# Top-32 attention and an ELU feed-forward on one core: remainder queries by four heads, and a planned feed-forward

## The chip, the core and the metric

The kernel runs on one core of a Trainium2 chip. Its time is the device time of that core in microseconds (us). The kernel before takes 1917.3 us, the median of three runs from 1916.89 to 1917.46. The core has a matrix engine (TensorE, PE in the profile), a vector engine (VectorE, DVE), a scalar engine (ScalarE, ACT), GpSimd (POOL) and DMA queues. Each engine works through its own list of instructions in order and waits on semaphores for the others.

## What is computed

Attention over 8 batches and 8 heads, 576 queries and 576 keys of width 64, in which each query keeps its 32 largest scores, and then a feed-forward with an ELU between its two matrices (512 to 2048 to 512) over the 4608 rows:

```python
scores = scale * np.matmul(q, k.transpose(0, 1, 3, 2))
kth = np.partition(scores, -top_k, axis=-1)[..., -top_k:-top_k + 1]     # top_k = 32
scores = np.where(scores >= kth, scores, -1000000000.0)
scores = scores - np.max(scores, axis=-1, keepdims=True)
attn = np.exp(scores)
attn = attn / (np.sum(attn, axis=-1, keepdims=True) + 1e-09)
x = np.matmul(attn, v)            # (B, H, S, D), then to rows of B*S, columns of H*D
h = x @ w_in
g = np.where(h > 0.0, h, np.exp(np.minimum(h, 0.0)) - 1.0)
out = g @ w_out
```

The two weight matrices arrive as float64 and are turned into fp32 in the kernel, from their bits.

## The kernel before

**Attention in steps.** 576 queries are four tiles of 128 (query tiles 0 to 3) and a remainder of 64 (tile 4). A step is one query tile and one pair of heads (hp, four pairs). In a full step each of the two heads has 128 rows of 576 scores. In a step of the remainder the two heads share the 128 partitions, 64 rows each, so there is only one such block (`nh = 1`, `weight = 0.5`). There are 8 batches of 16 full and 4 half steps, 160 in all, with 288 blocks of 128 x 576 to select from.

Step n goes through a software pipeline. `scores` (lines 243 to 266) is issued two steps ahead: per head two matmuls of 288 keys (L252) into PSUM, and ACT's scaled copy to SBUF (L261). `select` (L268) finds the 32nd largest: four MAX8 (L277, L287) and three MATCH_REPLACE8 (L281) per head on DVE. `mask` (L290) is issued a step later: two small operations on POOL (L298, L300), then a steep Prelu and an exp with a running sum on ACT (L301, L302). `normalise` (L306) takes a reciprocal on DVE (L311) and multiplies on POOL (L313). Two steps later `trans` (L317) turns four chunks of 128 keys per head with TensorE (L326) and copies them (L331), `trans_rest` (L336) turns the last 64 keys of each head on its own into 64 partitions (L341, L342), and `attend` (L347) multiplies by the values (L360) for a group of one or two query tiles, and copies the result into a block's `xT` (L377).

**Feed-forward in blocks.** A block is one to three tiles of 128 tokens, in which all 512 columns of x are wanted. The first pair of batches has blocks of 1, 1, 2, 2 and 3 tiles, every later pair three blocks of 3. When a block's last attention is in, `ffn_pieces` appends its work to a list: 16 hidden pieces (four matmuls each, L390, Relu and Exp on ACT, L398 and L399, and a gate on DVE, L400), and four projection pieces per tile (four matmuls of 512 columns each, L411). PSUM has two buffers for these pieces (`ps_f`).

**What sets the order.** The program is written step by step; a scheduler then orders each engine's instructions under the pools' buffers. `feed` is called four times in a step: it adds credit, 8 units per full step and at most 16 in store, and issues pieces while the credit covers them. A hidden piece costs as many units as its block has tiles, a projection piece 3.8. Nothing is issued until the weights are decoded (`"g" in late`).

**Decoding of the weights.** 32 pieces of 512 KB are loaded and decoded by `decode_piece`, three integer operations on DVE, four on ACT and two on POOL each (lines 144 to 168), called by `hook`, which `select` calls four times per head, eight per full step. Four buffers (`raw`) hold loads; after the last piece their space goes to the hidden activations (`g`).

Of the kernel before, what the change touches and what calls it, by code (L numbers as in the profile page):

```python
# [18 lines left out]
FEED = 8.0  # L19
# [17 lines left out]
class Block:  # L37


    def __init__(self, slots):  # L40
        self.slots = slots
        self.xT = None
        self.gT = []
        self.left = 0
        self.tiles = [[] for _ in range(slots)]
# [10 lines left out]
class Step:  # L56


    def __init__(self, t, hp, group, at):
        self.t, self.hp = t, hp  # L60
        self.group, self.at = group, at
        self.nh = 1 if t.rem else 2
        self.weight = 0.5 if t.rem else 1.0
# [3 lines left out]
def kernel(  # L67
# [44 lines left out]
    rawpool = raws.enter_context(tc.tile_pool(name="raw", bufs=4))  # L112
# [13 lines left out]
    def weight(i):  # L126
        per = dff // WN
        if i < NC * per:
            c, f = divmod(i, per)
            src = moe_w_in[c * P : (c + 1) * P, 2 * f * WN : 2 * (f + 1) * WN]  # L130
            return src, w_in[:, c, f * WN : (f + 1) * WN]
# [12 lines left out]
    def convert_first(i):  # L144
# [13 lines left out]
        nc.scalar.activation(e, ef, AF.Relu, scale=-(2.0**23), bias=span[:])  # L158
        nc.gpsimd.tensor_tensor(mf, mf, lof, ALU.add)
# [10 lines left out]
    decode = []  # L170

# [9 lines left out]
    def decode_piece(i):  # L181
        if i < 2 * NF:
            if i + 3 < 2 * NF:
                load_weight(i + 3)
            convert_first(i)
        if i > 0:
            convert_last(i - 1)

# [16 lines left out]
    def load_v(b, hp):  # L205
        t = kvpool.tile([P, 2, J + 1, D], FP32, tag="vT", name="vT")
        for hh in range(2):
            h = 2 * hp + hh
            nc.sync.dma_start(
                t[:, hh, 0:J, :],  # L210
                v[b, h, 0:JP, :].rearrange("(p j) d -> p j d", j=J),
            )
        nc.sync.dma_start(
            t[0:R, :, J, :],
            v[b, 2 * hp : 2 * hp + 2, JP:S, :].rearrange("h p d -> p h d"),
        )
# [26 lines left out]
    def scores(u):  # L243
        t = u.t
        kq = kqT[t.b, u.hp]
        q0 = t.qt * P
        u.sc = scpool.tile([P, 2, S], FP32, tag="sc", name="sc")
        ps = ps_sc.tile([P, 2, 2, 512], FP32, tag="s", name="scps")
        for half in range(2):
            for i in range(2):  # L250
                rows = slice(i * D, i * D + R) if t.rem else slice(0, P)
                nc.tensor.matmul(  # L252
                    ps[rows, i, half, 0:HS],
                    kq[i * D : (i + 1) * D, 1, q0 : q0 + t.ql],
                    kq[i * D : (i + 1) * D, 0, half * HS : (half + 1) * HS],
# [3 lines left out]
        for i in range(2):  # L259
            rows = slice(i * D, i * D + R) if t.rem else slice(0, P)  # L260
            nc.scalar.activation(  # L261
                u.sc[rows, 0 if t.rem else i, :].rearrange("p (a s) -> p a s", a=2),
                ps[rows, i, :, 0:HS],
                AF.Copy,
                scale=scale,
            )

    def select(u, i):  # L268
        if i >= u.nh:
            return  # L270
# [5 lines left out]
        hook()  # L276
# [3 lines left out]
        for r in range(TOP_K // 8 - 1):  # L280
# [7 lines left out]
            hook()  # L288

    def mask(u, i):  # L290

        if i >= u.nh:
            return
        if i == 0:
            u.den = small.tile([P, 2], FP32, tag="den", name="den")
        sc, low, top = u.sc[:, i, :], u.last[:, i, 7:8], u.first[:, i, 0:1]
# [9 lines left out]
    def normalise(u):  # L306
        nh = u.nh
        den = small.tile([P, 2], FP32, tag="dene", name="dene")
        nc.gpsimd.tensor_scalar_add(den[:, 0:nh], u.den[:, 0:nh], EPS)
        rec = small.tile([P, 2], FP32, tag="rec", name="rec")  # L310
        nc.vector.reciprocal(rec[:, 0:nh], den[:, 0:nh])  # L311
        for i in range(nh):
# [4 lines left out]
    def trans(u):  # L317

        g = u.group
        if g.et is None:  # L320
            n = len(g.tiles)
            g.et = etpool.tile([P, 2 * J + 2, n, P], FP32, tag="et", name="et")
        for i in range(u.nh):
            ps = ps_t.tile([P, JP], FP32, tag="t", name="eps")
            for c in range(J):
                nc.tensor.transpose(  # L326
                    ps[:, c * P : (c + 1) * P],
                    u.sc[:, i, c * P : (c + 1) * P],
                    ident[:],
                )  # L330
            nc.scalar.copy(  # L331
                g.et[:, i * J : (i + 1) * J, u.at, :],
                ps[:].rearrange("p (c q) -> p c q", c=J),
            )

    def trans_rest(u):  # L336

        g = u.group
        ps = ps_t.tile([P, JP], FP32, tag="t", name="eps")
        for i in range(u.nh):  # L340
            nc.tensor.transpose(ps[0:R, i * P : (i + 1) * P], u.sc[:, i, JP:S], ident[:])  # L341
        nc.scalar.copy(  # L342
            g.et[0:R, 2 * J : 2 * J + u.nh, u.at, :],
            ps[0:R, 0 : u.nh * P].rearrange("p (c q) -> p c q", c=u.nh),
        )

    def attend(g):  # L347
        t, hp = g.tiles[0], g.hp
        et, vt = g.et, vT[t.b, hp]
        n = sum(x.ql for x in g.tiles)  # L350
        ps = ps_t.tile([P, JP], FP32, tag="t", name="avps")
        for c in range(J + 1):
            for i in range(2):
                keys = slice(0, P if c < J else R)
                if t.rem:
                    w = et[keys, 2 * J if c == J else c, 0, i * R : (i + 1) * R]
                else:
                    w = et[keys, 2 * J + i if c == J else i * J + c, :, :]
                    w = w.rearrange("p a q -> p (a q)")
                nc.tensor.matmul(  # L360
                    ps[i * D : (i + 1) * D, 0:n],
                    vt[keys, i, c, :],
                    w,
                    start=(c == 0),
                    stop=(c == J),
                )
        c0 = 0
        tiles = list(g.tiles)
        while tiles:
            blk, lo = tiles[0].block, tiles[0].cols.start  # L370
# [199 lines left out]
```

## Time and profile before

| | before |
|---|---|
| time, median of 3 | 1917.3 us |
| span of the profiled run | 1915.4 us |
| TensorE busy | 1709.2 us, 89% |
| VectorE busy | 1615.8 us, 84% |
| ScalarE busy | 1169.8 us, 61% |
| GpSimd busy | 447.2 us, 23% |
| mean granted TensorE clock | 0.948 |
| hidden matmuls (L390) | 1792 instructions, 544.5 us |
| projection matmuls (L411) | 1152 instructions, 534.2 us |
| MAX8 and MATCH_REPLACE8 (L277, L281, L287) | 2016 passes of 754 to 761 ns |

The profile is one execution seen by the hardware profiler. A row of the timeline gives the start, the length, the engine, the line, the operation with its tiles and shapes, and in brackets how long the engine had been idle and what ended that. Matmuls overlap in the array, so the length of one matmul row says less than the distance from its start to the next row's start. A single-precision matmul is recorded as two instructions. The granted clock is the share of full speed at which TensorE ran.

### The profile page before, as it was taken

What the parts mean: (1) busy time and instruction counts of PE and PEld (TensorE: products, weight loads), DVE (VectorE), ACT (ScalarE), POOL (GpSimd) and SP (SyncE); (2) the same over time, 40 slices, a digit from 0 to 9 for tenths busy, and PEclk for the clock granted to TensorE, in tenths of its full rate; (3) what the DMA queues carried; (4) which work ended last, traced back from release to release, by engine and by line L of the source; (5) the groups of instructions that cost most, each with busy time, mean ns of one, the idle gap of its engine ahead of it and who ended that gap; (6) DMA issues with size and microseconds to landing.
All of it is one profiled execution on the core that took longest, in us unless ns stands there. A gap on an engine that the chain in (4) does not pass through costs nothing.

```text
span 1915.4 us, 24954 instructions
## 1 busy us (share of the span) xinstructions
PE 1709.2 (89%) x7984; PEld 946.7 (49%) x7984; DVE 1615.8 (84%) x3360; ACT 1169.8 (61%) x2453; POOL 447.2 (23%) x1096
## 2 busy tenths in 40 slices
PE   4028999999999999899989999999999999999999
PEld 2015656465554455455454455455555455445553
DVE  7999989999799998996999777997899777999310
ACT  6677667576666776575566466566566566557330
POOL 4774212222122222221222111221122211222000
PEclk7557999999899999999999999999999999999999
DMA  6430011000200110001100010000100000000000
GB/s 175 150 130 3 19 31 32 18 13 19 56 1 12 38 31 19 12 13 43 37 1 6 24 44 19 12 18 19 49 13 0 25 19 19 7 12 1 12 6 17
DMA packets 100610, 56.14 MB, mean 29 GB/s; under 512 B 83584, under 2 KB 91776, under 8 KB 100480
## 3 DMA queue, kind: packets, MB, share of 16 engines
q1 hardware_dynamic: 100480, 54.55, 10.3%
q8 instruction: 64, 1.05, 0.2%
q14 instruction: 66, 0.54, 0.1%
HBM read 45.09 MB, written 9.44 MB: 28 GB/s over the span
## 4 chain that ended last, share of the span: by engine, by line
DVE 56%; PE 31%; ACT 8%; issue 2%; POOL 1%; DMA 1%; SPq 0%; POOLq 0%; ACTq 0%; DVEq 0%
DVE wk L281 22%; DVE m L287 20%; PE hps L390 11%; PE ops L411 8%; DVE m L277 7%; PE scps L252 5%; PE avps L360 3%; DVE gT L400 3%; ACT sc L301 2%; PE eps L326 2%; ACT sc L261 2%; ACT sc L302 1%; DVE raw L164 1%; DVE raw L154 1%; DVE raw L151 1%
## 5 line engine op out<-in xcount | busy, mean ns | idle before, releaser
L287 DVE MAX8 m<-wk 128x8 f32<-128x576 f32 x864 | 631.9, 761 | 4.1
L390 PE MATMUL hps<-xT,w_in 128*128 128x384 f32 (+2 forms) x1792 | 544.5, 451 | 16.3 <-DVE gT L400 15.2
L411 PE MATMUL ops<-w_out,gT 128*128 128x512 f32 x1152 | 534.2, 604 | 0.0
L281 DVE MATCH_REPLACE8 wk<-m,wk 128x576 f32<-128x576 f32 x576 | 432.4, 754 | 0.0
L301 ACT ACTIVATE sc<-sc,neg 128x576 f32<-128x576 f32 x288 | 223.1, 775 | 336.5 <-POOL neg L298 336.0
L390 PEld LDWEIGHTS hps<-xT,w_in 128*128 128x128 f32 x1792 | 310.9, 192 | 196.0 <-DVE gT L400 31.0
L411 PEld LDWEIGHTS ops<-w_out,gT 128*128 128x128 f32 x1152 | 208.7, 192 | 223.1 <-issue 219.1
L252 PE MATMUL scps<-kqT 64*128 64x288 f32 (+1 forms) x1280 | 255.4, 456 | 17.4 <-ACT sc L261 15.8
L298 POOL TENSOR_SCALAR neg<-m 128x1 f32<-128x1 f32 x288 | 62.8, 218 | 847.2 <-DVE m L287 845.9
L277 DVE MAX8 m<-sc 128x8 f32<-128x576 f32 x288 | 215.7, 758 | 51.9 <-ACT sc L261 51.5
L313 POOL TENSOR_SCALAR sc<-sc,rec 128x576 f32<-128x576 f32 x288 | 214.0, 753 | 116.6 <-DVE rec L311 93.3
L302 ACT ACTIVATE sc<-sc,gap 128x576 f32<-128x576 f32 x288 | 223.4, 776 | 15.4 <-ACT sc L301 1.5
L360 PE MATMUL avps<-et,vT 128*64 128x256 f32 (+5 forms) x2000 | 205.9, 342 | 26.3 <-ACT et L342 25.6
L281 DVE MATCH_REPLACE8 wk<-m,sc 128x576 f32<-128x576 f32 x288 | 216.6, 754 | 0.0
L326 PE MATMUL eps<-ident,sc 128*128 128x128 f32 x1152 | 173.2, 284 | 48.1 <-ACT xT L377 23.5
L261 ACT ACTIVATE sc<-scps 128x576 f32<-128x576 f32 (+1 forms) x320 | 192.6, 641 | 28.9 <-PE scps L252 27.7
L400 DVE SCALAR_TENSOR_TENSOR gT<-n,hps 128x384 f32<-128x384 f32 (+2 forms) x224 | 109.9, 491 | 116.7 <-ACT n L399 115.0
L326 PEld LDWEIGHTS eps<-ident,sc 128*128 128x128 f32 x1152 | 133.4, 145 | 124.5 <-issue 70.7
L331 ACT COPY et<-eps 128x512 f32<-128x512 f32 x288 | 159.9, 585 | 51.4 <-PE eps L326 50.5
L360 PEld LDWEIGHTS avps<-et,vT 128*64 128x64 f32 (+1 forms) x2000 | 113.7, 141 | 135.2 <-issue 48.2
L252 PEld LDWEIGHTS scps<-kqT 64*128 64x128 f32 (+1 forms) x1280 | 121.0, 186 | 104.3 <-issue 58.2
L398 ACT ACTIVATE n<-hps 128x384 f32<-128x384 f32 (+2 forms) x224 | 98.3, 439 | 119.7 <-PE hps L390 118.1
(41 smaller groups left out, 969.1 us busy)
## 6 DMA issues: line engine op xcount, KB each, us to landing
kin<-in_k_dram SPq DMA_DIRECT2D x64, 128.0 KB, 2.7
qin<-in_q_dram SPq DMA_DIRECT2D x64, 128.0 KB, 2.8
raw<-in_moe_w_in_dram SPq DMA_DIRECT2D x16, 512.0 KB, 4.6
vT<-in_v_dram SPq DMA_DIRECT2D x64, 128.0 KB, 2.1
raw<-in_moe_w_out_dram SPq DMA_DIRECT2D x16, 512.0 KB, 3.2
out_dram<-osb SPq DMA_DIRECT2D x32, 256.0 KB, 2.3
kin<-in_k_dram SPq DMA_DIRECT2D x32, 32.0 KB, 2.5
qin<-in_q_dram SPq DMA_DIRECT2D x32, 32.0 KB, 2.5
```

Source lines behind the costliest of these rows:

```text
L252: nc.tensor.matmul(ps[rows, i, half, 0:HS], kq[i * D : (i + 1) * D, 1, q0 : q0 + t.ql], kq[i * D : (i + 1) * D, 0, half * HS : (half + 1) ...
L261: nc.scalar.activation(u.sc[rows, 0 if t.rem else i, :].rearrange("p (a s) -> p a s", a=2), ps[rows, i, :, 0:HS], AF.Copy, scale=scale,)
L277: nc.vector.max(m, sc)
L281: nc.vector.match_replace(wk[:], m, cur, TAKEN)
L287: nc.vector.max(m, cur)
L301: nc.scalar.activation(sc, sc, AF.Prelu, bias=neg[:], alpha=STEEP)
L302: nc.scalar.activation(sc, sc, AF.Exp, bias=gap[:], accum_out=u.den[:, i : i + 1])
L313: nc.gpsimd.tensor_scalar(u.sc[:, i, :], u.sc[:, i, :], rec[:, i : i + 1], 1.0, ALU.mult, ALU.mult)
L326: nc.tensor.transpose(ps[:, c * P : (c + 1) * P], u.sc[:, i, c * P : (c + 1) * P], ident[:],)
L360: nc.tensor.matmul(ps[i * D : (i + 1) * D, 0:n], vt[keys, i, c, :], w, start=(c == 0), stop=(c == J),)
L390: nc.tensor.matmul(ps[:, 0:n_tok], w_in[:, i, f * P : (f + 1) * P], blk.xT[:, i, 0:n_tok], start=(i == 0), stop=(i == NC - 1),)
L411: nc.tensor.matmul(blk.o[:], blk.gT[f // NG][:, f % NG, s * P : (s + 1) * P], w_out[:, f, :], start=(f == 0), stop=(f == NF - 1),)
```

## The change

Five things are changed together.

1. **Four heads per step of the remainder queries.** A step of tile 4 now takes four heads: two blocks of 128 rows, each made of 64 rows of one head and 64 of another. A batch has two such full steps instead of four half ones, 144 steps in all. `nh` and `weight` go.
2. **Last keys side by side.** Scores are taken as 512 keys and then 64 keys per head. The first head's last 64 keys and the second head's last 64 keys lie next to each other, so that nine chunks of 128 columns cover both heads; `turn` replaces `trans` and `trans_rest`, and nine wide transposes replace eight wide and two narrow ones.
3. **Blocks of two and three tiles.** The first pair of batches has blocks of 1, 1, 2, 1, 2 and 2 tiles, the later pairs 2, 2, 3 and 2; the remainder comes before the last two query tiles in every odd batch.
4. **A plan in place of the credit.** From the step at which each block becomes ready (`ready`) and the work of all blocks before it, `feed` computes the slowest rate that still finishes each block before the next is ready, and issues pieces at that rate. Costs are 1.1, 1.85 and 2.7 for a hidden piece of one, two and three tiles and 3.55 for a projection piece. Decoding is called half as often (four pieces per step), with the first matrix decoded column block by column block and three load buffers, and the first block may start on the weights decoded so far, with its own small buffer (`early`). The first eight steps run without the software pipeline's delay (`tight`).
5. **Gates queued late.** A hidden piece no longer issues its gate; it is put into `gates`, and issued when two are waiting, at the next `feed`, or before a projection.

The core of the diff:

```diff
+HIDDEN = {1: 1.1, 2: 1.85, 3: 2.7}
+PROJECT = 3.55
...
+        if t.rem:
+            rows = [(4 * hp, 0), (4 * hp + 2, 0), (4 * hp + 3, 1), (4 * hp + 1, 1)]
...
-    rawpool = raws.enter_context(tc.tile_pool(name="raw", bufs=4))
+    early = raws.enter_context(tc.tile_pool(name="early", bufs=1))
+    rawpool = raws.enter_context(tc.tile_pool(name="raw", bufs=3))
...
-        ps = ps_sc.tile([P, 2, 2, 512], FP32, tag="s", name="scps")
-        for half in range(2):
-            for i in range(2):
+        ps = ps_sc.tile([P, 4 * JP], FP32, tag="s", name="scps")
+        first = (0, 3 * JP - R)
+        main = (0, 3 * JP)
+        rest = (JP, 3 * JP - R)
+        for start, keys in ((main, slice(0, JP)), (rest, slice(JP, S))):
+            for h, i, rows in u.heads:
...
             nc.vector.max(m, cur)
-            hook()
+            if r != 1:
+                hook()
+                yield
...
+    def turn(u, chunks):
...
+        for c in range(n):
+            c0 = (chunks.start + c) * P
+            nc.tensor.transpose(ps[:, c * P : (c + 1) * P], sc[:, c0 : c0 + P], ident[:])
...
+            if len(gates) > 1:
+                close_gates()
             ps = ps_f.tile([P, dm], FP32, tag="f", name="hps")
...
-            nc.vector.scalar_tensor_tensor(
-                out=blk.gT[f // NG][:, f % NG, 0:n_tok],
-                in0=n[:, 0:n_tok], scalar=-1.0, in1=ps[:, 0:n_tok],
-                op0=ALU.add, op1=ALU.max,
-            )
+            gates.append((blk.gT[f // NG][:, f % NG, 0:n_tok], n, ps))
...
-            sizes = (1, 1, 2, 2, 3) if b == 0 else (3, 3, 3)
+            division = [(0,), (1,), (2, 3), (rest,), (4, 5), (6, 7)]
+            if b > 0:
+                division = [(0, 1), (2, 3), (rest, 4, 5), (6, 7)]
...
-        credit[0] = min(credit[0] + FEED * share * u.weight, 2 * FEED)
-        while ffn and credit[0] >= ffn[0][0]:
-            cost, piece = ffn.pop(0)
-            credit[0] -= cost
+        close_gates()
+        fed["at"] = max(fed["at"], n)
+        ahead = [(w - fed["sum"]) / (x - fed["at"]) for x, w in due if x > fed["at"]]
+        if ahead:
+            fed["over"] += max(0.0, share * min(ahead))
+        fed["at"] += share
+        while ffn and decoded[0] >= ffn[0][1] and 0.5 * ffn[0][0] <= fed["over"]:
+            cost, _, piece = ffn.pop(0)
+            fed["over"] -= cost
+            fed["sum"] += cost
             piece()
...
+        if n < tight:
+            for i in range(2):
+                passes = choose(n, i)
+                next(passes)
+                if i == 0:
+                    while closing:
+                        attend(closing.pop(0))
+                elif prev:
+                    normalise(prev)
+                    turn(prev, slice(0, J))
+                    turn(prev, slice(J, J + 1))
+                    turn(prev, slice(J + 1, 2 * J + 1))
+                feed(n, 0.25)
+                next(passes)
+                mask(cur, i)
+                feed(n, 0.25)
+            continue
```

## The prediction

> **What bounds the kernel now.** I read the page's first two parts, then the busy time of each engine in five stretches, then the order in time of TensorE around three moments, and last what VectorE waited for.
>
> ```profile
> PE 1709.2 (89%) x7984; PEld 946.7 (49%) x7984; DVE 1615.8 (84%) x3360; ACT 1169.8 (61%) x2453; POOL 447.2 (23%) x1096
> ...
> PE   4028999999999999899989999999999999999999
> ...
> DVE  7999989999799998996999777997899777999310
> ...
> PEclk7557999999899999999999999999999999999999
> ```
>
> TensorE (PE) is nearly empty in the first four slices and full afterwards; VectorE (DVE) is full in the first slices, has holes later and is empty for the last two. So one of them limits the start and the other the rest.
>
> ```profile
> 0.00:190.00 190.00, 72.14 (x395) 48.24 (x396) 174.06 (x291) 131.96 (x255) 111.65 (x129) 0.64 0.39 115
> 190.00:255.00 65.00, 64.76 (x369) 41.96 (x367) 63.30 (x149) 41.02 (x109) 15.30 (x43) 1.00 0.05 14
> 255.00:518.00 263.00, 252.51 (x1352) 151.49 (x1351) 239.03 (x521) 179.63 (x390) 57.10 (x167) 0.97 0.12 30
> 518.00:1787.00 1269.00, 1196.17 (x5448) 642.06 (x5447) 1124.67 (x2374) 788.32 (x1641) 260.83 (x754) 0.98 0.07 19
> 1787.00:1916.00 129.00, 123.61 (x426) 62.93 (x426) 14.70 (x28) 28.87 (x62) 2.29 (x6) 1.00 0.04 13
> ```
>
> Columns: PE, PE weight load, DVE, ACT, POOL busy, granted clock, DMA. The cuts are the moments at which 32, 80 and all 288 head-selections had been scored. PE idles 118 us up to 190, where weight decoding fills DVE; then 11 us to 518, 73 us of 1269 in the long stretch, 5 in the tail. In the long stretch DVE has 144 us free. The tail is feed-forward alone.
>
> ```profile
> 1014.30 1.24 PE L252 MATMUL scps<-kqT 64*128 64x288 f32 x8
> 1015.47 2.53 PE L360 MATMUL avps<-et,vT 128*64 128x256 f32 x20
> 1017.93 2.85 PE L390 MATMUL hps<-xT,w_in 128*128 128x384 f32 x8
> 1020.61 1.35 PE L326 MATMUL eps<-ident,sc 128*128 128x128 f32 x8
> ...
> 1080.99 3.70 PE L411 MATMUL ops<-w_out,gT 128*128 128x512 f32 x8
> 1084.53 1.04 PE L326 MATMUL eps<-ident,sc 128*128 128x128 f32 x8
> ...
> 1098.67 0.70 PE L252 MATMUL scps<-kqT 64*64 64x288 f32 x4
> 1101.52 0.66 PE L226 MATMUL qkps<-ident,qin 128*128 128x128 f32 x4 [2.15 <-ACT et L342]
> ...
> 1103.52 2.93 PE L390 MATMUL hps<-xT,w_in 128*128 128x384 f32 x4
> 1106.24 1.91 PE L326 MATMUL eps<-ident,sc 128*128 128x128 f32 x8
> ```
>
> Each fp32 matmul shows as two instructions, a transpose as one. Start to start is the real price: scores of a full step 1.17 us, attention of two tiles 2.46, a hidden piece of three tiles 2.68, a projection piece 3.54. No gap lies between them: PE is saturated there. The last rows are in the remainder steps of one batch: a gap of 2.15 us, and then a hidden piece takes 2.72 (1103.52 to 1106.24), where four matmuls are half a piece, 1.34.
>
> ```profile
> 1205.25 0.76 DVE L277 MAX8 m<-sc 128x8 f32<-128x576 f32 x1
> ...
> 1214.95 0.76 DVE L277 MAX8 m<-sc 128x8 f32<-128x576 f32 x1
> ```
>
> Undisturbed, a step costs DVE 9.7 us without gates.
>
> ```profile
> DVE rec L311 <- POOL dene L309: 64.3, 36, 4.1
> DVE m L277 <- ACT sc L261: 51.5, 38, 6.2
> DVE gT L400 <- ACT n L399: 46.8, 40, 2.6
> ```
>
> Between 190 and 1797 us DVE waits 163 us, mostly for results of an ACT that itself waits for PE. Order of limits, then: DVE to about 500 us, PE after.
>
> **What the Trainium skill says.** "TensorE: Matmul & The Clock Gate", What's actually happening: an idle window of about 3.4 us halves the matmul clock, and work must last as long again to restore it. The trace agrees in kind: clock 0.50 from 40 to 120 us, and 0.72 at 810-820 us after a gap of 3.52 us. "TensorEngine Tiling (Array Packing)", Key Properties: separate tiles of the array run in parallel. It agrees: two score matmuls on the two halves of the array take 0.64 us (four instructions from 1111.17 to 1111.81), one alone 0.63 (two from 1109.52 to 1110.15). "Perfetto Trace Analysis", Identifying the Most-Contended Engine: matmul busy time is a poor distance from the roof. It agrees: 255-518 us shows 252 busy, while the counted work below is 222. "VectorE: DVE Perf Modes", section on the TRN2 errata: a fixed cost per instruction. The gates show 548, 415 and 284 ns for 384, 256 and 128 columns, so about 150 ns fixed.
>
> **The change part by part.** Counts are from the built order of both programs.
>
> *Blocks of two.* 14 blocks (2 of one tile, 2 of two, 10 of three) become 18 (3, 12, 3). A hidden piece costs 1.02, 1.86, 2.68 us for one, two, three tiles (from x16 rows in 2.05, x8 in 1.83 to 1.92, x8 in 2.68). Before 16 x (2 x 1.02 + 2 x 1.86 + 10 x 2.68) = 521; after 16 x (3 x 1.02 + 12 x 1.86 + 3 x 2.68) = 535: PE +14. Projection is unchanged, 144 pieces. Gates: 110 to 120 us on DVE (192 at 415 ns, 48 each at 548 and 284), +10, inside DVE's 144 free us. ACT's two passes: +24 us, inside its idle 39%.
>
> *Keys side by side.* 1152 wide and 288 narrow transposes become 1296 wide ones. A lone narrow pair costs 0.31 us (1024.39 to 1024.70), one more wide transpose 0.11: PE -16 (144 x 0.11) to -26 (128 x 0.2); I take -21. One copy of 128x128 (0.27) replaces 64x256 (0.36): ACT relief, hidden.
>
> *Scores of 512 + 64 keys.* Columns are equal, and fitting rows of 64 and 256 columns (20 in 0.88 and 2.46 us) prices both forms at 1.17 us when the four matmuls stand together. But where other work falls between the two heads, the pairing is lost: 0.57 us for 288 columns (0.63 + 1.11 - 1.17), about 0.95 for 512. In the order I find some 22 such splits in full steps before and 39 after (39 x 0.95 - 22 x 0.57 = +24), 19 and 7 in remainder steps (7 x 0.95 - 19 x 0.57 = -4). PE +20. Sum of PE work: 14 - 21 + 20 = +13, from +4 to +22.
>
> *Four heads per remainder step.* 32 half steps (4.9 us of DVE each) become 16 full ones; selections stay 288. Half steps leave the chain mask, exponential, normalise, transpose, which is two steps long, half the time; there sit gaps of 1 to 3.5 us on PE, followed by half clock. I count about 2.5 us of gap and as much clock loss per batch: 8 x 5 = 40, most of it removable. Estimate -15 to -30.
>
> *Decoding spread.* 33 pieces at 8 per step become 4 per step. DVE work is the same 93 us, and DVE is full either way, so its step 14 stays near 250 us (12 until the first max, 93 decode, 14 x 9.7, 9 of gates). The first block may use weights early, but the order shows it gives PE less: at 32 selections scored, feed-forward issued is 61 us before and 36 after. At 80 it is equal (178 both), and until there DVE limits. Cost 0 to +10: PE must not fall behind between. I take +3.
>
> *Plan and late gates.* Per 16 selections in the long stretch feed-forward ran 30 to 71 us before; after 55 to 64. Other PE work is 35 per 16, DVE 78 plus 6 of gates. The bin of 30 was DVE-bound (81 against 65), that of 71 held DVE back for 21 (106 against 85). After, every bin has PE at 90 to 99 and DVE at 84: PE never starves by plan. Bin by bin the larger of the two sums to 1209 before against 1196 of PE work alone, so evenness recovers about 13 of the 73 us. Late gates add a wait: hidden piece f+2 needs its buffer, hence gate f, queued behind selection passes of 0.7 us each; other PE work stands between. PE waited 15 us on it before. Estimate -10 to +10, 0 taken. Plan: -13.
>
> *Tail.* After the last score 118 us of feed-forward stood in PE's order before and 120 stand after, so the smaller last block does not shorten a PE-bound end: 0.
>
> Sum: 1917 + 13 - 22 + 3 - 13 + 0 = 1898.
>
> **The rivals.**
> *The gaps nearly vanish.* PE at 255 us for 32 selections, 262 for the next 48, 1203 / 0.985 = 1221 for the rest, 130 tail: 1868. For it: even feeding, no half steps. Against: about 40 PE waits of 0.4 to 2.5 us lie outside the remainder steps, each from in-order queues that stay.
> *Nothing moves.* PE work grows by as much as gaps shrink: 1917. For: PE holds at its limit for 1400 us whatever is fed.
> *Slower.* Splits, late gates and late feed cost, and two engines close to full stall each other: the 73 us of gaps stay, PE +22, start +5: 1944. For: 25 us less feed-forward done at 255 us, and two psum buffers with deferred gates. Against: DVE keeps 10% free.
>
> **How the numbers follow.** Forecast 0.44, gaps vanish 0.20, nothing moves 0.13, slower 0.23. The range 1866 to 1938 takes the best case in and cuts the slower one near its middle. Within 0.2% of 1917.3 is 1913.5 to 1921.1: 0.10. Faster 0.64, slower 0.26.
>
> **What would show it.** Right: long stretch with PE idle under 50 us of some 1250, granted clock nearer 1.0 with no dips at batch ends, waits of the reciprocal and of the first max shrunk, PE busy a little up. Wrong: PE idle at the gate's wait growing past 30 us; score rows with one 512 matmul alone at 1.0 us, over 50 of them; the time of 32 scored selections past 270 us; or DVE idle before 500 us.

## The result, and the profile after

| | before | after |
|---|---|---|
| time, median of 4 runs each, same chip | 1917.1 us | 1874.2 us (1872.26 to 1875.2) |
| ratio, 95% interval | 1 | 0.9776 (0.9759 to 0.9793) |
| TensorE busy, idle (profiled span) | 1709.2, 206.2 us (1915.4) | 1719.2, 154.2 us (1873.4) |
| TensorE busy in hidden, projection rows | 544.5, 534.2 | 576.5, 539.1 |
| in rows of scores, transposes of attention weights, attention | 255.4, 230.3, 205.9 | 261.1, 207.7, 205.0 |

The change saves 43 us where 19 were forecast. One slow execution in the whole study, of the kernel with the plan (2476.7 us at a granted clock of 0.648), is left out of every figure. The page of the changed kernel, first two parts:

```profile
PE 1719.2 (92%) x8352; PEld 1033.6 (55%) x8352; DVE 1608.4 (86%) x3408; ACT 1143.9 (61%) x2505; POOL 439.6 (23%) x1080
...
PE   4457999999999999999999999899998999899999
...
DVE  7899999999999998989889888988989888898400
...
PEclk7556999999999999999999999999999999999999
```

The holes of VectorE in the middle are smaller (eights and nines where there were sixes and sevens) and the row of the granted clock has lost its one dip past the start. Finer windows still show dips in the changed kernel (columns: TensorE, its weight loads, VectorE, ScalarE, GpSimd, clock, DMA):

```profile
330.00:340.00 10.00, 8.59 (x27) 5.74 (x30) 7.80 (x18) 4.27 (x10) 2.19 (x6) 0.66 0.00 0
```

TensorE is less empty in the first four slices, at half clock.

The busy time by stretches of the changed kernel, cut where 32, 80 and all 288 selections had been scored (same columns):

```profile
0.00:231.00 231.00, 153.82 (x684) 95.24 (x685) 206.35 (x400) 164.03 (x344) 121.29 (x161) 0.69 0.34 99
231.00:500.00 269.00, 261.70 (x1410) 160.25 (x1410) 262.68 (x585) 181.04 (x409) 62.31 (x179) 0.99 0.11 29
500.00:1742.00 1242.00, 1176.82 (x5817) 705.61 (x5816) 1118.27 (x2381) 763.91 (x1677) 252.18 (x732) 0.98 0.07 19
1742.00:1874.00 132.00, 126.88 (x448) 72.46 (x446) 21.09 (x45) 34.90 (x79) 3.83 (x9) 1.00 0.03 10
```

The long stretch went from 1264 or 1269 us (the cut moves by a step's length) to 1242, but TensorE's idle time in it only from 73 to 65: most of that gain is shorter busy time. Before the second cut 18 to 23 us were won. The tail is the same length, 132 against 129.

What VectorE waited for from 190 to 1742 us of the changed kernel:

```profile
DVE rec L330 <- POOL dene L328: 67.0, 31, 2.8
DVE m L291 <- ACT sc L281: 30.8, 30, 2.5
DVE gT L409 <- ACT n L438: 22.3, 32, 1.9
```

The reciprocal waits as long as before (64.3), the first max (51.5) and the gate (46.8) for 45 us less together. VectorE waits less, but TensorE sets the end, so this alone proves nothing.

### The profile page after: what moved, and what is told of

The parts are those of the page before. It is cut to its first block, busy times and chain, and to the rows that moved or that the text cites. A ratio compares the mean times of both kernels' runs of the same rounds, so it can differ in the third digit from the quotient of the medians.

```text
span 1873.4 us, 25844 instructions
## 1 busy us (share of the span) xinstructions
PE 1719.2 (92%) x8352; PEld 1033.6 (55%) x8352; DVE 1608.4 (86%) x3408; ACT 1143.9 (61%) x2505; POOL 439.6 (23%) x1080
## 4 chain that ended last, share of the span: by engine, by line
DVE 61%; PE 21%; ACT 11%; issue 3%; POOL 1%; DMA 1%; SPq 0%; POOLq 0%; ACTq 0%; DVEq 0%
DVE wk L295 25%; DVE m L301 22%; DVE m L291 8%; PE hps L429 7%; PE ops L447 7%; ACT sc L318 4%; DVE gT L409 3%; PE scps L273 3%; ACT sc L319 3%; ACT sc L281 2%; PE avps L375 2%; PE eps L348 2%; DMA raw<-in_moe_w_in_dram 1%; DVE raw L168 1%; DVE raw L182 1%
## 5 line engine op out<-in xcount | busy, mean ns | idle before, releaser
L429 PE MATMUL hps<-xT,w_in 128*128 128x256 f32 (+2 forms) x2304 | 576.5, 397 | 35.2 <-DVE gT L409 34.9
L447 PE MATMUL ops<-w_out,gT 128*128 128x512 f32 x1152 | 539.1, 608 | 0.0
L429 PEld LDWEIGHTS hps<-xT,w_in 128*128 128x128 f32 x2304 | 408.3, 198 | 152.7 <-DVE gT L409 59.4
L349 ACT COPY et<-eps 128x512 f32<-128x512 f32 (+1 forms) x432 | 193.5, 475 | 154.1 <-PE eps L348 153.6
L273 PE MATMUL scps<-kqT 64*128 64x64 f32 (+3 forms) x1280 | 261.1, 464 | 16.2 <-ACT sc L281 15.7
L348 PE MATMUL eps<-ident,sc 128*128 128x128 f32 x1296 | 207.7, 284 | 58.6 <-ACT et L349 19.6
L348 PEld LDWEIGHTS eps<-ident,sc 128*128 128x128 f32 x1296 | 160.8, 145 | 176.0 <-issue 60.2
L291 DVE MAX8 m<-sc 128x8 f32<-128x576 f32 x288 | 209.6, 749 | 32.8 <-ACT sc L281 30.8
L375 PE MATMUL avps<-et,vT 128*64 128x256 f32 (+5 forms) x2000 | 205.0, 337 | 9.1 <-ACT et L349 8.8
L409 DVE SCALAR_TENSOR_TENSOR gT<-n,hps 128x256 f32<-128x256 f32 (+2 forms) x288 | 118.1, 411 | 106.6 <-ACT n L438 105.3
L437 ACT ACTIVATE n<-hps 128x256 f32<-128x256 f32 (+2 forms) x288 | 109.3, 380 | 151.5 <-PE hps L429 150.3
L281 ACT ACTIVATE sc<-scps 128x576 f32<-128x576 f32 x288 | 170.6, 640 | 13.3 <-PE scps L273 13.2
```

The lines of the kernel that those rows point to most:

```text
L273: nc.tensor.matmul(ps[rows, start[i] : start[i] + keys.stop - keys.start], kq[part, 1, q0 : q0 + u.t.ql], kq[part, 0, keys], start=True, s ...
L281: nc.scalar.activation(u.sc[:, i, :], ps[:, first[i] : first[i] + S], AF.Copy, scale=scale)
L291: nc.vector.max(m, sc)
L348: nc.tensor.transpose(ps[:, c * P : (c + 1) * P], sc[:, c0 : c0 + P], ident[:])
L375: nc.tensor.matmul(ps[i * D : (i + 1) * D, cols], vt[rows, 2 * J if c == J else i * J + c, :], w, start=(c == 0), stop=(c == J),)
L429: nc.tensor.matmul(ps[:, 0:n_tok], w_in[:, i, f * P : (f + 1) * P], blk.xT[:, i, 0:n_tok], start=(i == 0), stop=(i == NC - 1),)
```

## The experiments

All were timed beside the kernel before on the same chip. The chips' kernels before lay between 1916.3 and 1918.3 us, so pieces are compared by their ratios, each times 1917 us; an interval of one ratio is about 3 us to each side, of a difference of two about 4.

### Parts 1 and 2 alone, built up from the kernel before

*Four heads per remainder step, with the attention of the remainder written for four heads and the loads timed for 18 steps per batch, nothing else:*

```diff
-        self.nh = 1 if t.rem else 2
-        self.weight = 0.5 if t.rem else 1.0
+        self.nh = 2
+        self.weight = 1.0
+        if t.rem:
+            rows = [(4 * hp, 0), (4 * hp + 2, 0), (4 * hp + 3, 1), (4 * hp + 1, 1)]
...
-            for i in range(2):
+            for h, i, rows in u.heads:
```

> The kernel before with four heads per remainder step alone (keys still in halves of 288, narrow transposes kept, loads timed for 18 steps per batch). Theory P1 (the remainder steps are most of the gain: scores of four heads run in four quarters of the array at once, some 20 us less TensorE work, and the gaps of the half steps go): 1875 to 1892. Rival P2 (wide transposes are most of it): 1900 to 1918. Rivals C and S: 1905 to 1920.

Measured: 1883.49 us, 0.9826 (0.981 to 0.984): -33 us, the greater part of the whole change. The groups of the remainder's scores, first in the kernel before, then in this one (busy us, mean ns of an instruction, idle before):

```profile
L252 PE MATMUL scps<-kqT 64*64 64x288 f32 x256 | 56.3, 424 | 0.0
```

```profile
L259 PE MATMUL scps<-kqT 64*64 64x288 f32 x256 | 29.9, 437 | 0.0
```

The same 256 instructions of nearly the same length fill half the time. The order in time shows why, before (a half step) and here (a step of four heads):

```profile
1089.16 1.19 PE L252 MATMUL scps<-kqT 64*64 64x288 f32 x8
```

```profile
449.13 1.20 PE L259 MATMUL scps<-kqT 64*64 64x288 f32 x16
```

A half step has two heads, so two 64x64 quarters of the array work at a time; a step of four heads has all four at work, and its sixteen instructions take as long as the eight did. Whole half steps alone would fill only 32 x 1.11 = 36 of the 56.3 us, though. In 23 of the 32, other work falls in between, as here before, and the parts take 0.62 and 1.11 us from start to start:

```profile
466.02 0.69 PE L252 MATMUL scps<-kqT 64*64 64x288 f32 x2
466.64 0.27 PE L234 MATMUL qkps<-ident,kin 64*128 64x64 f32 x1
...
466.91 1.18 PE L252 MATMUL scps<-kqT 64*64 64x288 f32 x6
```

Of the steps of four heads 9 of 16 are split. So about 17 of the 26 us are the four quarters (36 - 16 x 1.13), the rest fewer splits and the clock. The page:

```profile
PE 1680.0 (89%) x7984; PEld 937.3 (50%) x7984; DVE 1611.4 (86%) x3344; ACT 1141.1 (61%) x2389; POOL 441.8 (24%) x1080
```

TensorE's busy time fell by 29 us (from 1709.2: all scores -19, transposes -6, attention -6), its idle time by only 7 (206.2 to 1879.6 - 1680.0 = 199.6). About 7 of the 29 are lower clock, by the estimate given with the plan below. ScalarE's 64 evictions of 64 partitions (41.2 us) became 32 of 128 partitions, and its busy time fell by 29 us.

*Part 1 with keys side by side:*

```diff
-        for half in range(2):
+        for start, keys in ((main, slice(0, JP)), (rest, slice(JP, S))):
...
-    def trans(u):
-    def trans_rest(u):
+    def turn(u, chunks):
```

> Only the first two parts of the change (four heads per remainder step, last keys side by side): decoding eight times per step with its old order of operations and buffers, no early block, no steps without the pipeline's delay, blocks of 1, 1, 2, 2, 3 and then of 3, credit, gates at once. Theory P (the gain is in these two parts): 1850 to 1880. Rival C (no part alone, but plan, blocks and late gates together): 1900 to 1920. Rival S (the start): 1895 to 1920.

Measured: 1886.58, 0.9843 (0.983 to 0.986), +3 us on part 1, about nothing: transposes 223.9 to 207.3 us, scores 236.4 to 264.8. Under that near zero lie two larger movements: TensorE's busy time rose by 23 us (1680.0 to 1702.6) and its idle time fell by 18 (199.6 to 181.9).

*Is it work, or gaps? Remainder scores issued twice, on part 1:*

```diff
-            for h, i, rows in u.heads:
+            for h, i, rows in u.heads * (2 if t.rem else 1):
```

> The kernel before with four heads per remainder step alone, in which each score matmul of a remainder step is issued twice (the second writes the same values again; nothing else changes): 16 groups of 8 matmuls more, which took about 1.2 us as a group of 16 instructions, so some 19 us of TensorE work. If time follows TensorE work one to one (theory: that is where the 34 us of this part came from), 1883.5 + 15 to 20 = about 1900. If the gain came from gaps at the half steps and TensorE has room there, the doubled work fills gaps: 1890 or less.

Measured: 1923.56, 1.0037 (1.0025 to 1.0049), 40 us more than part 1. The row grew by 18.6 us, as it should:

```profile
L259 PE MATMUL scps<-kqT 64*64 64x288 f32 x512 | 48.5, 451 | 0.0
```

So TensorE has no room to hide 19 us: added work does not vanish in gaps. But 40 is twice the added work: busy time rose by 28, to 1707.8 (some 8 of it lower clock by the estimate below), and idle time by 15 (1922.5 - 1707.8 = 214.7). The scheduler had ordered much of TensorE's list anew. What that did by itself is not separated, so this run shows the sign and not a price.

*Can the quarters be made to run one after another? Part 1, each head's two halves written next to each other:*

```diff
-        for half in range(2):
-            for h, i, rows in u.heads:
+        order = [(half, x) for half in range(2) for x in u.heads]
+        if t.rem:
+            order = [(half, x) for x in u.heads for half in range(2)]
+        for half, (h, i, rows) in order:
```

> The kernel before with four heads per remainder step (as in the run at 1883), but in a remainder step the two halves of one head's keys follow each other, so that neighbours in TensorE's list want the same quarter of the array. Same work, same steps. Theory Q (four heads gain because their score matmuls run in four quarters at once: 26 us less of them): the remainder scores take 45 to 60 us busy and not 30, time 1898 to 1912. Rival H (they gain because half steps and their gaps are gone): 1880 to 1888.

Measured: 1886.22, 0.9837 (0.982 to 0.985). Fourteen instructions still took 1.22 us (1.19 in part 1) and the group 32.1: the quarters were not serialised, so the test missed its purpose. Whether the scheduler kept the written order is not known, so it says nothing on the order either.

### Plan, blocks and decoding, one at a time on parts 1 and 2 (1886.6 us)

*The plan in place of the credit:*

```diff
-        fed["over"] = min(fed["over"] + FEED * share, 2 * FEED)
+        ahead = [(w - fed["sum"]) / (x - fed["at"]) for x, w in due if x > fed["at"]]
+        if ahead:
+            fed["over"] += max(0.0, share * min(ahead))
```

> The kernel with the first two parts alone (1886.6 us), and the plan in place of the credit, nothing else. Of the 12 us between it and the changed kernel the plan as predicted would bring 13: about 1874. In the changed kernel the credit in its place was 5 us faster than the plan: by that about 1890. The late-start theory (the rest is from the start) expects 1886 within 4.

Measured: 1865.3, 0.9733 (0.972 to 0.975): -21 us, the largest gain after the four heads. The first line of the page, without the plan and with it:

```profile
PE 1702.6 (90%) x7840; PEld 931.8 (49%) x7840; DVE 1610.2 (85%) x3344; ACT 1133.1 (60%) x2389; POOL 439.3 (23%) x1080
```

```profile
PE 1679.0 (90%) x7840; PEld 924.0 (50%) x7840; DVE 1604.3 (86%) x3344; ACT 1134.3 (61%) x2389; POOL 440.0 (24%) x1080
```

As many instructions, 24 us less busy, and the idle time is unchanged: 181.9 (1884.5 - 1702.6) and 182.6 (1861.6 - 1679.0). Half of the 24 is in the score rows (264.8 to 252.6). Those of 512 keys in full steps, without the plan and with it:

```profile
L272 PE MATMUL scps<-kqT 64*128 64x512 f32 x512 | 204.0, 677 | 15.5 <-ACT sc L280 13.3 <-ACT kqT L249 2.0
```

```profile
L271 PE MATMUL scps<-kqT 64*128 64x512 f32 x512 | 192.0, 668 | 16.2 <-ACT sc L279 14.1 <-ACT kqT L248 2.0
```

The mean of one fell by 1%, the time that they fill by 6%: more of them overlap. From 250 us on, the order in time has about 47 rows in which one 512-key matmul stands alone without the plan, and about 28 with it. The rest is 2 to 4 us each in keys, projection and attention.

Another part is the clock. After a gap a row can take twice as long, and this counts as busy time. Without the plan, with the granted clock at 0.50 (490 to 495 us), such a lone matmul takes 2.00 us from start to start, and soon after 1.05:

```profile
489.55 1.30 PE L348 MATMUL eps<-ident,sc 128*128 128x128 f32 x5 [1.69 <-ACT kqT L249]
490.78 2.07 PE L272 MATMUL scps<-kqT 64*128 64x512 f32 x2
492.78 1.11 PE L348 MATMUL eps<-ident,sc 128*128 128x128 f32 x4
...
501.17 1.12 PE L272 MATMUL scps<-kqT 64*128 64x512 f32 x2
502.22 0.66 PE L348 MATMUL eps<-ident,sc 128*128 128x128 f32 x4
```

An estimate of what the clock costs is TensorE's busy time in windows of 5 us, from 250 to 1850 us, each times the share of the clock that was not granted:

| kernel | us |
|---|---|
| before; four heads; four heads with scores doubled | 28; 21; 29 |
| parts 1 and 2; with plan; with blocks; with decoding | 26; 12; 35; 35 |
| changed kernel; with credit; without early block | 21; 36; 13 |
| best version | 9 |

By this about 14 of the plan's 24 us are clock. The profiled execution with the plan has a mean granted clock of 0.957; two others, at 0.951 and 0.952, took 4 to 5 us longer, so their share may be smaller.

*Blocks of two and three, remainder ahead of the last tiles in odd batches:*

```diff
-            division = [(0,), (1,), (2, 3), (4, 5), (6, 7, rest)]
-                division = [(0, 1, 2), (3, 4, 5), (6, 7, rest)]
+            division = [(0,), (1,), (2, 3), (rest,), (4, 5), (6, 7)]
+                division = [(0, 1), (2, 3), (rest, 4, 5), (6, 7)]
```

> The kernel with the first two parts alone (1886.6 us), and the changed kernel's blocks (1, 1, 2, 1, 2, 2 tiles, then 2, 2, 3, 2) with the remainder ahead of the last two tiles in odd batches, nothing else. As predicted 14 us more of TensorE work: 1900. If the blocks are ready earlier and so fill gaps, and this is the 12 us: about 1875.

Measured: 1895.99, 0.9893 (0.988 to 0.991): +10 us. Hidden rows went from 544.5 to 556.9 us, but all busy time only from 1702.6 to 1707.0; idle time rose by 8, to 189.6.

*Decoding spread, no early block:*

```diff
-    rawpool = raws.enter_context(tc.tile_pool(name="raw", bufs=4))
+    rawpool = raws.enter_context(tc.tile_pool(name="raw", bufs=3))
...
-            hook()
             if r != 1:
+                hook()
                 yield
```

> The kernel with the first two parts alone (1886.6 us), and the decoding of the changed kernel: four pieces per step, column blocks first, three load buffers, the addition after the last of the piece before, nothing else; the first block still waits for all weights. As predicted up to 10 us slower, 1887 to 1897; if the shorter decoding passes (16 us less on VectorE in the start) are the 12 us: about 1872.

Measured: 1882.25, 0.9816 (0.980 to 0.983): -5 us. The three decoding passes on VectorE, without the new decoding (41.9 + 29.0 + 23.7 = 94.6 us) and with it (27.3 + 24.5 + 22.6 = 74.4):

```profile
L168 DVE TENSOR_SCALAR raw<-raw 128x512 uint32<-128x512 uint32 x32 | 41.9, 1308 | 0.0
L183 DVE SCALAR_TENSOR_TENSOR raw<-raw 128x512 uint32<-128x512 uint32 x32 | 29.0, 906 | 0.0
L165 DVE TENSOR_SCALAR raw<-raw 128x512 uint32<-128x512 uint32 x32 | 23.7, 742 | 11.9 <-DMA raw<-in_moe_w_in_dram 11.9
```

```profile
L183 DVE SCALAR_TENSOR_TENSOR raw<-raw 128x512 uint32<-128x512 uint32 x32 | 27.3, 853 | 2.4 <-ACT raw L173 2.4
L166 DVE TENSOR_SCALAR raw<-raw 128x512 uint32<-128x512 uint32 x32 | 24.5, 766 | 19.4 <-DMA raw<-in_moe_w_in_dram 16.9 <-DMA raw<-in_moe_w_out_dram 1.0 <-POOL w_in L187 0.9
L169 DVE TENSOR_SCALAR raw<-raw 128x512 uint32<-128x512 uint32 x32 | 22.6, 707 | 0.0
```

20 us less on the engine that limits the start, and 5 at the end: most of it is not passed on.

Added up: -33 + 3 - 21 + 10 - 5 = -46, and the changed kernel has -43. That would leave 3 us of cost for late gates, the eight tight steps and the early block, if the pieces added. They do not: the early block and the tight steps alone, taken out together, are worth 12 (last experiment).

### Pieces taken back from the changed kernel (1874.2 us, 0.9776)

*Decoding at eight pieces per step, first block after all weights; then the second edit alone:*

```diff
+        hook()
         nc.vector.max(m, sc)
...
-        behind = 2 * NF if blk.number else 0
+        behind = 2 * NF
```

> The changed kernel with the decoding pieces called eight times per step again, as before, and the first block fed only when all weights are decoded. Theory S (the gain I did not forecast comes from the start: VectorE's decode passes are held up less by GpSimd when they are spread, 77 us against 93, and TensorE gets work while they run): decode passes near 90 us, 80 selections scored some 15 to 25 us later, time 1888 to 1898. Rival L (the gain comes from the long stretch: plan and late gates): 1870 to 1878. Rival P (it comes from less TensorE work: remainder scores and wide transposes): 1870 to 1878.

> The changed kernel with decoding spread as in it, but the first block waits for all weights like the others. Theory S: decode passes stay near 77 us, but feed-forward starts some 60 us later and bursts, time 1879 to 1889; with the run at eight per step this splits the start into its two parts. Rivals L and P: 1870 to 1878.

Measured: 1871.22 (0.9772) with both, 1860.31 (0.9708, 0.969 to 0.972) with the second alone. The early block costs 13 us. With that block late, eight decoding pieces per step in place of four cost 11 (1871.22 against 1860.31): here the spread decoding gains, and the early block gives that back. The hidden rows of one tile in the first 250 us, of the changed kernel and then without the early block:

```profile
L429 PE MATMUL hps<-xT,w_in 128*128 128x128 f32 x242 | 45.1, 343 | 12.9 <-DVE gT L409 12.7
```

```profile
L426 PE MATMUL hps<-xT,w_in 128*128 128x128 f32 x248 | 37.8, 303 | 0.5 <-DVE gT L409 0.5
```

Fed early into a stretch at half clock (0.53 from 60 to 120 us), the same work takes 7 us longer and waits 12 for its gates. Past 250 us the estimate of lost clock is 21 with the early block and 13 without, which may be the larger part of the 13; it is not traced to single waits.

*Gates at once; credit in place of the plan:*

```diff
             gates.append((blk.gT[f // NG][:, f % NG, 0:n_tok], n, ps))
+            close_gates()
```

```diff
-            fed["over"] += max(0.0, share * min(ahead))
...
+        fed["over"] = min(fed["over"] + FEED * share, 2 * FEED)
```

> The changed kernel with each gate issued at once behind its hidden piece. Theory S: 1870 to 1882, gates matter little. Rival L: VectorE waits at the gates grow (from 21 us between the start and the tail towards 50) and the time is 1888 to 1900. Rival P: 1870 to 1880.

> The changed kernel with the old credit (8 units per step, at most 16, a piece costs as many units as its block has tiles, 3.8 for a projection piece) in place of the plan. Theory S: 1872 to 1884. Rival L: 1888 to 1905, bursts of hidden matmuls while VectorE waits. Rival P: 1870 to 1880.

Measured: 1867.6 (0.9748, 0.973 to 0.976) and 1868.84 (0.9762, 0.974 to 0.978): neither the late gates nor the plan helps *here*, though the plan gives 21 us on parts 1 and 2. Past 250 us the plan saves as much clock as there (36 us lost with the credit, 21 with the plan). But the credit here also feeds before all weights are decoded, from the first block on, and keeps the clock of the start higher. All score rows up to 250 us with the credit (clock 0.80; 0.71 in the changed kernel, next fences):

```profile
0.00:250.00 250.00, 51.52 (x168) 0.80 0.33 95
```

The same estimate for these 250 us is 27 us lost with the credit, 45 with the plan. So the plan's gain is likely lost again at the start; no run takes the two apart.

*Blocks of three again; the addition on GpSimd earlier, as before; no tight steps:*

```diff
-                division = [(0, 1), (2, 3), (rest, 4, 5), (6, 7)]
+                division = [(0, 1, 2), (3, 4, 5), (rest, 6, 7)]
```

```diff
         nc.scalar.activation(e, ef, AF.Relu, scale=-(2.0**23), bias=span[:])
+        nc.gpsimd.tensor_tensor(mf, mf, lof, ALU.add)
```

```diff
-    blocks, tight = [], 2 * NHP
+    blocks, tight = [], 0
```

> The changed kernel with blocks of three tiles in all pairs of batches but the first. Theory P (TensorE bound, so its work decides: hidden pieces of three tiles cost 0.89 us per tile against 0.93): about 9 us less TensorE work, 1860 to 1870. Rival C (blocks of two feed evenly): 1880 to 1900.

> The changed kernel with GpSimd's add of a decode piece issued with the piece's first operations, as before, and not after the product of the piece ahead. If the order on GpSimd is what makes VectorE's decode passes shorter, they sum to 88 to 95 us and not 77. Theory P: time 1872 to 1880. Rival S: 1885 to 1895.

> The changed kernel with the first eight steps in the same pipeline as the others (mask a step later, transposes two). Undoing early block, decoding rate, late gates, plan or blocks one by one each left the time the same or shorter, yet all of them together are worth 12 us over the first two parts alone. Theory D (the direct order of the first eight steps is what brings the start forward): 32 selections scored near 260 us and not 227, time 1885 to 1915. Rival E (nothing single; only order noise of the scheduler): 1868 to 1880.

Measured: 1868.65 (0.9751), 1873.92 (0.9778), 1863.91 (0.9723, 0.971 to 0.974). Blocks of three gain 5 here; the addition's place is worth nothing; the tight steps cost 10. All score rows up to 250 us, of the changed kernel and then without tight steps:

```profile
0.00:250.00 250.00, 54.98 (x162) 0.71 0.32 93
```

```profile
0.00:250.00 250.00, 41.44 (x168) 0.73 0.33 94
```

Without them six instructions more take 13.5 us less: with tight steps about 12 rows of one 512-key matmul stand alone in this stretch, most at 2.0 us, without them about 3, at 1.05. (Columns after the busy time: clock, DMA.)

### Towards the best version

*First block late, gates at once, blocks of three:*

```diff
-        behind = 2 * NF if blk.number else 0
+        behind = 2 * NF
...
+            close_gates()
...
+                division = [(0, 1, 2), (3, 4, 5), (rest, 6, 7)]
```

> The changed kernel with all weights decoded before the first block, gates at once, and blocks of three tiles from the second pair of batches on: the three single edits that each came out faster. If they add up: 1845 to 1855. If they are one and the same slack, or the scheduler's noise: 1856 to 1868.

Measured: 1862.45 (0.9721, 0.971 to 0.973), no better than the first of the three alone: single gains of 5 us do not add.

*Parts 1 and 2, plan and decoding, with none of the rest; beside it the changed kernel without early block and tight steps:*

```diff
-    blocks, tight = [], 2 * NHP
+    blocks, tight = [], 0
-        behind = 2 * NF if blk.number else 0
+        behind = 2 * NF
```

In the first of the two also:

```diff
+            close_gates()
...
+            division = [(0,), (1,), (2, 3), (4, 5), (6, 7, rest)]
+                division = [(0, 1, 2), (3, 4, 5), (6, 7, rest)]
+        order = [(0, 1), (2, 3), (J,)]
```

> The changed kernel without its blocks of two and three (before's 1, 1, 2, 2, 3 and then 3, 3, 3, remainder last in every batch), without late gates, without the eight tight steps, and with the first block waiting for all weights: four heads, keys side by side, plan and decoding alone. If the terms measured on the first two parts add up (1886.6 - 19 - 4), 1863, and the pieces left out cost the changed kernel 11 us. If the plan and the decoding need the early block or the blocks of two, 1870 or more.

> The changed kernel without the eight tight steps and with the first block waiting for all weights; blocks of two and three and late gates stay. Each alone was 10 and 14 us faster; if they add, 1850; if they remove the same loss at the start, about 1860. Against the kernel beside it in this call it prices blocks of two and late gates under the plan: as predicted 14 us slower than it.

Measured: 1857.01 (0.9671, 0.966 to 0.969) and 1864.15 (0.9712, 0.970 to 0.973). The first is the best kernel of the study, 20 us under the changed one and 63 under the one before. Its page:

```profile
PE 1682.3 (91%) x7840; PEld 930.8 (50%) x7840; DVE 1582.9 (86%) x3344; ACT 1135.3 (61%) x2389; POOL 445.7 (24%) x1080
```

Compared with the changed kernel TensorE is busy 37 us less and idles 14 more (1850.0 - 1682.3 = 167.7). This profiled execution is the fastest of the four, 1851.79 at a clock of 0.958. Between the two lie 8 us for blocks of two with late gates, and between the second and the changed kernel 12 for the early block and the tight steps.

## Why the prediction was right or wrong

The direction held, and the sense of nearly every term; the sum was too small by 24 us.

| term of the forecast | forecast | measured | from |
|---|---|---|---|
| four heads, with its part of the splits | -22 - 4 = -26 | -33 | part 1 alone |
| keys side by side, with splits | -21 + 24 = +3 | +3 | part 2 on part 1 |
| plan | -13 | -21 | plan on both |
| blocks of two | +14 | +10 | blocks on both |
| decoding, early block, late gates, tight steps | +3 + 0 | -5 + 3 = -2 | decoding on both; the 3 is what is left of the sum, not measured |
| sum | -19 | -43 | |

*The step that failed is "Four heads per remainder step".* It priced the remainder's score matmuls at the same time as before but for 4 us ("Columns are equal") and put the gain, 22 us, on gaps in the half steps and half clock after them. In that run gaps gave 7 of the profiled 36 us and clock, by estimate, another 7; the remainder's score rows, with some of that clock in them, gave 26. I had cited the rule that separate tiles of the array run in parallel and had measured it on pairs, 0.64 us for two against 0.63 for one; I did not carry it to quarters. The Trainium skill, "TensorEngine Tiling (Array Packing)", The Solution, lists 64x64 as four independent tiles. The runs agree: 16 instructions in 1.20 us on four quarters, 8 in 1.19 on two. The working was there to do: 32 half steps x 1.11 = 36 us would become 16 x 1.13 = 18. All scores together fell by only 19.0 us: the remainder's rows by 26, while those of full steps rose by 7, with about 40 rows of a lone matmul past 250 us where there were 22. Doubling the remainder's scores made the kernel 40 us slower, so they are on the path.

*The split into work and gaps agrees by luck.* Taken whole, TensorE's busy time rose by 10 us (+13 forecast) and its idle time fell by 52 (32 forecast), as if only the gaps had been mis-sized. The pieces built up say otherwise: busy time -29 with four heads, +23 with the new keys, -24 with the plan, and the early block and tight steps added 35 (1684.4 without them), 26 of it before 250 us, at low clock. The best version has more idle time than the changed kernel and is 20 us faster.

*Plan: right sign, wrong mechanism.* I let evenness recover idle time of TensorE. It recovered none (181.9 and 182.6) and took 24 us of busy time: by estimate 14 through fewer stretches at half clock, and the rest mostly through fewer splits (about 47 lone rows, then 28). I had counted such splits for the new keys, and held them fixed when I changed the feed. In the changed kernel taking the plan back costs nothing, probably because it loses at the start what it gains later.

*Keys and splits: the sum right, in part by luck.* On part 1, transposes fell by 17 us where 16 to 26 were forecast, and scores rose by 28 for +24. But busy time rose by 23 in all and 18 us of idle time went, which was not forecast. In the changed kernel full steps' scores are also up by about 28 (199.1 to 227, which is 261.1 less 26.6 + 7.2 of the remainder), but that is another sum: without the tight steps all scores are 243.8.

*Blocks of two: right in size.* Hidden rows rose by 12.4 us alone, +14 forecast, though part of this is lower clock (26 to 35 us by the estimate, over all rows). In the changed kernel they rose by 32, 8 of it because of the early block (568.4 without); the rest is not traced singly.

*Decoding and start: sign wrong, size small.* I took VectorE's 93 us of decoding as fixed. They became 77.1 in the changed kernel and 74.4 alone. The early block, though, was a loss of 13, past the 0 to 10 named.

*Late gates 0: near.* TensorE's wait for a gate rose from 15.2 to 34.9 us, past the 30 named as a sign of failure; 12.7 of it in the early block. Taking late gates back alone gained 5 us.

*Tail 0: right,* 129 and 132. *What would show it:* clock dips gone, no (28 us lost before, 21 after, by the estimate); reciprocal's wait shrunk, no (64.3 and 67.0); first max's, yes; TensorE busy a little up, yes, by the luck named above; long-stretch idle under 50 us, no (65): that was the sign that the gain was not in gaps. Of the other signs of being wrong, rows of a lone 512-key matmul number about 50, at the limit named; 32 selections were scored at 231 us, not past 270; VectorE idled 31 us to 500, and 42 to 518 before. The rival of vanishing gaps gave 1868, nearest to the time of 1874.2, for the wrong reason: idle time past the first cut fell only from 89 us (262 us on, before) to 78 (231 us on, after). One reading of the prediction is to be corrected: the row from 1103.52 has four instructions, which are two matmuls, half a hidden piece; its half clock stands.

## What to carry to other kernels

Before you look for gaps, count how many parts of the matrix array a group of small matmuls keeps busy: four 64x64 problems together cost what two do here, and such a gain shows as less busy time, not as less idle time. Busy time also holds the half clock, so look at the clock in fine windows before calling it work. A feed that interleaves other work with such groups changes their price, so count the split groups anew for each change of the order. A change of several pieces should be built up piece by piece as well as taken apart: of the pieces taken back from the changed kernel nearly every one looked idle or harmful; built up, two of them held the gain, and leaving the late gates, the blocks, the early block and the tight steps out gave the best version. Each price here includes what the scheduler made of that one edit (40 us for 19 us of added work), so prices of 5 to 13 us do not carry to another kernel.

## What the hardware showed that I had not expected

*Half clock after short gaps.* In the lines shown with the plan, TensorE had waited for 1.69 us before 489.55, and the clock was then 0.50 until 495. That gap is shorter than the idle window of about 3.4 us that the prediction names.

*Long decoding passes.* VectorE's plain decoding passes (TENSOR_SCALAR) take 0.4 us or, in most other cases, 1.5. All 43 decoding passes over 1 us in the kernel before begin during a GpSimd operation; so do 17 of the 53 shorter ones. From the kernel before:

```profile
64.03 0.41 DVE L151 TENSOR_SCALAR raw<-raw 128x512 uint32<-128x512 uint32 x1
64.25 1.31 POOL L168 TENSOR_TENSOR w_in<-raw 128x512 f32<-128x512 f32 x1 [0.69 <-DVE raw L164]
64.37 1.48 DVE L154 TENSOR_SCALAR raw<-raw 128x512 uint32<-128x512 uint32 x1
```

The pass from 64.37 on ends at 65.85, 0.29 us after the GpSimd multiply at 65.56; the one ahead of it took 0.41. The Trainium skill, "SBUF — State Buffer", Who interferes with whom, says that GpSimd and some VectorE operations share a pair of ports under an exclusive lock, held for the whole instruction, and the later one waits. The trace agrees with that. In the kernel before 43 of 96 passes took over 1 us, in the changed one 25, all of them begun during a GpSimd operation too. Which part of the new decoding does that is open: the place of the addition changed little (74.3 us against 77.1), and eight pieces per step instead of four with the new order took 73.2.
